# An S5 scan beside a GeGLU on one core: third row block of w_up loaded before x's third tile, and that tile summed by two engines and turned later

## The chip, the cores and the metric

The kernel runs on one core of a Trainium2 chip. The time is device microseconds of one execution; what is compared is the median of several. The kernel before was run three times: 178.42, 178.84 and 178.85 us, median 178.84. A profile is one more execution, with every engine's instructions recorded: TensorE (PE, its weight loads PEld), VectorE (DVE), ScalarE (ACT), GpSimd (POOL), and SyncE (SP), which here issues every transfer.

## What is computed

x is 2048 tokens by 512 channels, in bf16. The normalised x goes through two branches, a diagonal complex recurrence over the tokens (S5) and a gated feed-forward net, and the two are multiplied and added to x:

```python
def _layernorm(x, axis=-1, eps=1e-5):
    m = jnp.mean(x, axis=axis, keepdims=True)
    v = jnp.var(x, axis=axis, keepdims=True)
    return (x - m) / jnp.sqrt(v + eps)
...
    Bu = jnp.einsum("bld,pd->blp", x + 0j, B_bar)
    for t in range(L):
        h = Lam_bar[None, :] * h + Bu[:, t, :]
    y = 2.0 * jnp.einsum("blp,dp->bld", hseq, Cmat).real + x * Dskip[None, None, :]
...
def _B_ref(x, w_gate, w_up, w_down):
    return (_gelu(x @ w_gate) * (x @ w_up)) @ w_down
...
    xn = _layernorm(x, axis=-1)
    s = _A_ref(xn, ...)
    g = _silu(_B_ref(xn, B_w_gate, B_w_up, B_w_down))
    return x + s * g
```

w_gate and w_up are 512 by 1376, w_down is 1376 by 512.

## The kernel before

The tokens are worked in four slabs of 512, each of four tiles of 128 tokens. For each slab the kernel makes the gate and up products, their product turned by a transposing DMA (atT), the product with w_down, the projection by B, the scan (VectorE), and the projection by C. Everything is a step in a list, and the step numbers in the table ORDER fix the order of the instructions: each engine runs its own instructions strictly in that order. SP does the same with the transfers, so a transfer that waits holds back all that are issued behind it.

The change lies in the head, the first 11 us, where slab 0 has to start before x and the weights are all there. x's tiles 0 to 3 (`load_x`, L221) and the 128-row blocks of w_up (`load_w`, L210; its first 1024 columns) are loaded one after the other, in the order x0, x1, w_up block 0, block 1, x2, block 2, block 3; then three small parameter vectors (pv, L234), w_up's other columns, x3 and w_gate. The transfers take their completion semaphores in turn from eight (DMAHW0 to DMAHW7), so a later one waits for the one eight places earlier.

For tiles 0 to 2 the mean is taken off first (`center`, L335), so that the products can start before the variance is known; the variance's factor rs is applied when the products leave PSUM. `center` of tile 0 splits the token sum between ScalarE (192 columns) and VectorE (320 columns). For tiles 1 and 2 ScalarE sums all 512 columns (L350) and VectorE subtracts (L351). `squares` (L354) sums the squares on ScalarE. TensorE turns the centred tile (`head_t`, L305, its transposes L328 into two PSUM banks, which VectorE and ScalarE copy into W, L330 and L331). Then come the row products (`up_rows`, L383): a step `up_rows(m, k)` multiplies tile m's k-th 128 channels with block k of w_up, two 128x512 matmuls into two banks, accumulated over k. There are twelve such steps for the three tiles. Between them lies the parameters' turn (L604: pv against an identity), whose result VectorE copies out (pf, L606), and from which GpSimd makes dt (L607) and later rho (L611) by powers, and VectorE the angles of the rotation tables. GpSimd also makes rs for each tile (L289 to L292). With tile 3's rs VectorE scales tile 3 (L360), and SP issues the first transposing DMA (xnT, L367), behind it those of B (BT, L240), of the first gate product (atT, L468), and the load of w_down (wd, L684).

After the row products TensorE goes on with w_up's last 352 columns and with w_gate (`first_w`, matmuls L421), then with the projection by B (L550) and the product with w_down (L484).

Of the kernel before, what the change touches and what calls it, by code (L numbers as in the profile page):

```python
# [10 lines left out]
AF = mybir.ActivationFunctionType  # L11
# [7 lines left out]


ORDER = (
# [23 lines left out]
)  # L45


# [33 lines left out]
def kernel(  # L81
# [46 lines left out]
    def sb(name, shape, dt=BF16):  # L128
        return consts.tile(shape, dt, name=name)
# [80 lines left out]
    def load_w(nm, k0, k1, c0, c1, end, landed):  # L210

        w, r = w_of[nm]
        dma_sp(end, landed, lambda: nc.sync.dma_start(out=w[:, k0:k1, c0:c1], in_=r[:, k0:k1, c0:c1]),  # L213
               [(nm, k, c) for k in range(k0, k1) for c in range(3) if c0 <= CH[c][0] < c1])
# [6 lines left out]
    def load_x(m, end, landed):  # L221
        dma_sp(end, landed, lambda: nc.sync.dma_start(out=x_tok[:, m, :], in_=x_r[:, m, :]), [("x", 0, m)])  # L222
# [4 lines left out]
    load_x(1, 1.59, 3.31)  # L227
    load_w("wu", 0, 1, 0, W2, 2.06, 4.3)
    load_w("wu", 1, 2, 0, W2, 2.53, 5.0)
    load_x(2, 3.0, 5.3)  # L230
    load_w("wu", 2, 3, 0, W2, 3.5, 6.0)
    load_w("wu", 3, 4, 0, W2, 4.0, 6.7)
    for i, v in enumerate((A_log_dt, A_Lambda_im, A_Lambda_re)):
        dma_sp(4.4 + 0.4 * i, 7.0, lambda i=i, v=v: nc.sync.dma_start(out=pv[4 * i : 4 * i + 4, :], in_=v.rearrange("(k p) -> k p", p=P)), [("pv", i)])  # L234
# [37 lines left out]
    nb = sb("nb", [P, NS, M], FP32)  # L272
    ma = sb("ma", [P, M], FP32)
    mb = sb("mb", [P, 1], FP32)
    ss = sb("ss", [P, M], FP32)

    def stats(m):
# [57 lines left out]
    def center(m):  # L335

        x = x_tok[:, m, :]
        if m == 0:
            c = 320
            acts(D - c, lambda: act(out=junk()[:, 0 : D - c], in_=x[:, c:D], func=AF.Copy, scale=1.0 / D, accum_out=mb[:, 0:1]),  # L340
                 [("x", 0, 0)], ["mb"], ptr=1, rank=400.0)
            dve(c, lambda: V.tensor_scalar(out=yg[0][:, 0:c], in0=x[:, 0:c], scalar1=1.0 / D, scalar2=None, op0=ALU.mult, op1=ALU.add,
                                           accum_out=ma[:, 0:1]), [("x", 0, 0)], [("yg", 0, 0), ("ma", 0)], base=0.15, rank=400.0, after=early)
            for i in range(2):
                hc = slice(i * HD, (i + 1) * HD)
                head.append(dve(256, lambda hc=hc: V.tensor_scalar(out=xn[0][:, hc], in0=x[:, hc], scalar1=ma[:, 0:1], scalar2=mb[:, 0:1], op0=ALU.subtract, op1=ALU.subtract),
                                [("x", 0, 0), ("ma", 0), "mb"], [("xc", 0, i)], rate=2.3, rank=400.0, after=head[-1:]))
            return
        nmean, key = ma[:, m : m + 1], ("ma", m)
        sums0.append(acts(512, lambda: act(out=junk()[:], in_=x, func=AF.Copy, scale=-1.0 / D, accum_out=nmean), [("x", 0, m)], [key], ptr=2, rank=400.0 - 20 * m))  # L350
        dve(512, lambda: V.tensor_scalar(out=xn[m], in0=x, scalar1=nmean, scalar2=None, op0=ALU.add),  # L351
            [("x", 0, m), key], [("xc", m, 0), ("xc", m, 1)], rate=2.3, rank=330.0 - 20 * m)
# [492 lines left out]
```

## Time and profile before

| | |
|---|---|
| median of three runs | 178.84 us (178.42 to 178.85) |
| the profiled execution's own time | 178.47 us |
| its span | 176.7 us |
| TensorE busy | 171.4 us, 97% |
| VectorE busy | 156.7 us, 89% |
| ScalarE busy | 124.0 us, 70% |
| GpSimd busy | 11.3 us, 6% |

The span runs from the first to the last recorded instruction; the execution's own time is 1.8 us longer. Times in the profile are us from the span's start. A row of a timeline reads: start, length, engine, line, operation, what it writes from what it reads, shapes, how many are merged; in brackets how long the engine was idle before and what ended that. Matmuls are pipelined, so the length of a merged row includes the last one's drain, and the pace is read from the distance of starts. "SPq" is SP issuing a transfer; how long the transfer takes until its completion is seen is told apart from that, as the time from issue to landing.

### The profile page before, as it was taken

The page shows a single profiled execution, that of the slowest core. Times are in us where ns is not written, and L with a number is a line of the kernel's source. Part 1 is how long each engine was busy: PE and PEld are TensorE (multiplying, and loading weights), DVE is VectorE, ACT ScalarE, POOL GpSimd, SP SyncE. Part 2 cuts the span into 40 slices and gives each one's busy share as a digit, 9 for nine tenths or more (in the row PEclk, how much of TensorE's full clock was granted, in tenths as well). Part 3 has the DMA queues.
Part 4 walks back from the last instruction along what each step waited for, and adds up shares of the span by engine and source line. Part 5 has one row for each costly group of instructions (what it writes and reads, how often), then busy time and mean ns, then how long its engine had stood idle before and what let it go on. Part 6 is the DMA issues. An engine that isn't in the chain of part 4 may idle for free.

```text
span 176.7 us, 2407 instructions
## 1 busy us (share of the span) xinstructions
PE 171.4 (97%) x830; PEld 82.1 (46%) x846; DVE 156.7 (89%) x254; ACT 124.0 (70%) x238; POOL 11.3 (6%) x25
## 2 busy tenths in 40 slices
PE   8999999999999999999999999999999999999992
PEld 2454554444455544444455454444444455444451
DVE  3578999999799994999979999899999999999764
ACT  5679989959999999799578855373158618582240
POOL 2282030000200000000040000000000000000000
PEclk9999999999999999999999999999999999999999
DMA  5999999999000809423000074194000006526112
GB/s 164 292 334 252 171 221 293 219 256 191 0 0 0 200 7 182 99 83 57 0 0 6 31 148 83 34 189 85 0 0 0 0 30 145 83 57 136 42 59 77
DMA packets 48355, 18.66 MB, mean 106 GB/s; under 512 B 40312, under 2 KB 47832, under 8 KB 48344
## 3 DMA queue, kind: packets, MB, share of 16 engines
q1 hardware_dynamic: 48344, 18.52, 48.2%
q8 instruction: 6, 0.10, 0.2%
q14 instruction: 5, 0.04, 0.1%
HBM read 6.46 MB, written 2.10 MB: 48 GB/s over the span
## 4 chain that ended last, share of the span: by engine, by line
PE 93%; DMA 2%; DVE 1%; SPq 1%; issue 1%; DVEq 0%
PE ring L452 31%; PE ring L484 21%; PE ring L550 16%; PE ybank L500 15%; PE ring L421 5%; PE ybank L421 2%; DMA wu<-in_B_w_up_dram 2%; PE ring L391 2%; DVE yg L505 1%; SPq L222 1%; DVE junk L511 1%; SPq L213 0%; PE ring L328 0%; DVEq L505 0%; PE ybank L604 0%
## 5 line engine op out<-in xcount | busy, mean ns | idle before, releaser
L452 PEld LDWEIGHTS <-xnT 128*128 128x128 bf16 x288 | 28.2, 98 | 28.4
L484 PE MATMUL ring<-wd,atT 128*128 128x512 bf16 (+1 forms) x171 | 38.9, 379 | 0.3
L452 PE MATMUL ring<-wg,xnT 128*128 128x512 bf16 (+1 forms) x142 | 31.4, 356 | 0.1
L452 PE MATMUL ring<-wu,xnT 128*128 128x512 bf16 (+1 forms) x142 | 31.2, 356 | 0.1
L550 PE MATMUL ring<-xnT,BT 128*128 128x512 bf16 x128 | 30.1, 379 | 0.0
L581 DVE TENSOR_TENSOR_SCAN Fs<-rho,ini,W 128x512 bf16<-128x512 f32 x24 | 29.7, 1271 | 0.1
L455 ACT ACTIVATE ub<-ring 128x512 bf16<-128x512 f32 (+1 forms) x36 | 19.2, 555 | 13.6 <-PE ring L452 13.5
L500 PE MATMUL ybank<-C,hst 128*128 128x512 bf16 x115 | 27.3, 379 | 0.3
L484 PEld LDWEIGHTS <-atT 128*128 128x128 bf16 (+1 forms) x176 | 17.2, 98 | 20.8
L552 ACT ACTIVATE U<-ring 128x512 bf16<-128x512 f32 x32 | 18.1, 599 | 7.5 <-PE ring L550 7.5
L455 ACT ACTIVATE gt<-ring 128x512 bf16<-128x512 f32 (+1 forms) x36 | 19.5, 555 | 3.7 <-PE ring L452 3.5
L500 PEld LDWEIGHTS <-hst 128*128 128x128 bf16 x136 | 13.3, 98 | 14.0
L487 ACT ACTIVATE g<-ring 128x512 f32<-128x512 f32 x16 | 9.4, 595 | 14.2 <-PE ring L484 14.2
L550 PEld LDWEIGHTS <-BT 128*128 128x128 bf16 x128 | 12.5, 98 | 14.7
L562 DVE TENSOR_TENSOR Q<-U,tab 128x4096 bf16<-128x4096 bf16 x8 | 18.3, 2290 | 0.9 <-ACT tab L646 0.7
L562 DVE TENSOR_TENSOR Q<-Fs,tab 128x4096 bf16<-128x4096 bf16 x8 | 18.3, 2287 | 0.1
L505 DVE TENSOR_TENSOR yg<-ybank,g 128x512 bf16<-128x512 f32 x15 | 10.2, 685 | 5.8 <-PE ybank L500 5.7
L763 ACT ACTIVATE junk<-x_tok 128x512 bf16<-128x512 bf16 x16 | 10.0, 631 | 1.5 <-DMA x_tok<-in_A_x_dram 1.5
L496 ACT ACTIVATE ybank<-sk 128x512 f32<-128x512 bf16 x15 | 9.0, 603 | 1.7 <-DVE yg L505 1.6
L768 ACT ACTIVATE xna<-x_tok,nb,rs 128x512 bf16<-128x512 bf16 x12 | 9.6, 813 | 0.0
L581 DVE TENSOR_TENSOR_SCAN Fs<-rho,W 128x512 bf16<-128x512 f32 x8 | 9.3, 1210 | 0.1
L461 DVE TENSOR_TENSOR at<-gt,ub 128x1024 bf16<-128x1024 bf16 x12 | 8.2, 684 | 0.0
(143 smaller groups left out, 170.2 us busy)
## 6 DMA issues: line engine op xcount, KB each, us to landing
x_tok<-in_A_x_dram SPq DMA_DIRECT2D x3, 512.0 KB, 4.4
out_dram<-ot SPq DMA_DIRECT2D x12, 128.0 KB, 2.1
wd<-in_B_w_down_dram SPq DMA_DIRECT2D x1, 1280.0 KB, 6.9
wu<-in_B_w_up_dram SPq DMA_DIRECT2D x4, 256.0 KB, 3.6
wg<-in_B_w_gate_dram SPq DMA_DIRECT2D x1, 864.0 KB, 7.2
x_tok<-in_A_x_dram SPq DMA_DIRECT2D x4, 128.0 KB, 4.2
wg<-in_B_w_gate_dram SPq DMA_DIRECT2D x1, 512.0 KB, 5.2
wu<-in_B_w_up_dram SPq DMA_DIRECT2D x1, 352.0 KB, 4.7
```

Of the source, the lines that this page charges most:

```text
L421: T.matmul(ps[:, 0 : b - a], lhsT=lhs(k), rhs=wt[:, k, a:b], start=(k == 0), stop=(k == KT - 1))
L452: T.matmul(ps[:, 0 : b - a], lhsT=xnT[:, s % 2, m, k, :], rhs=wt[:, k, a:b], start=(k == 0), stop=(k == KT - 1))
L455: acts(b - a, lambda: act(out=dst[:, a:b], in_=ps[:, 0 : b - a], func=AF.Copy if up else AF.Gelu_apprx_tanh), [("bank", r)], [key], table= ...
L484: T.matmul(ps[:], lhsT=atT[:fs, k, m * P : (m + 1) * P], rhs=wd[:fs, k, :], start=(k == 0), stop=(k == NFT - 1))
L500: T.matmul(ps, lhsT=hst[s % 2][:, j // NPT, j % NPT, m * P : (m + 1) * P], rhs=C2[:, j // NPT, j % NPT, c0:c1], start=(j == 0 and not seed ...
L505: dve(w, lambda: V.tensor_tensor(out=yg[e][:, c0:c1], in0=ps, in1=g2[gi][:, b, c0:c1], op=ALU.mult), [key, ("g2", gi, b)], [("yg", e, c0)])
L550: T.matmul(ps[:], lhsT=BT[:, ri, k, pt * P : (pt + 1) * P], rhs=xnT[:, s % 2, :, k, :], start=(k == 0), stop=(k == KT - 1))
L552: acts(512, lambda q=q, ri=ri, ps=ps: act(out=U[ui][:, ri, q, :], in_=ps[:], func=AF.Copy), [("bank", r)], [("U", ui, q, ri)])
L562: dve(4096, lambda: V.tensor_tensor(out=Qf, in0=src.unsqueeze(1).to_broadcast(WQ), in1=table, op=ALU.mult), reads, ["Q"], rate=2.0)
L581: pl.add(DVE, 1.12 if s == 0 else 1.185, lambda ri=ri, q=q, pt=pt, first=first: V.tensor_tensor_scan(out=Fs[:, ri, q, :], data0=rho[:, pt ...
L763: acts(512, lambda i=i, fn=fn, sc=sc, m=m: act(out=junk()[:], in_=x_tok[:, s * M + m, :], func=fn, scale=sc, accum_out=sx[:, s, i, m : m + ...
L768: acts(512, lambda m=m: act(out=xn[m], in_=x_tok[:, s * M + m, :], func=AF.Identity, scale=rs[:, s, m : m + 1], bias=nb[:, s, m : m + 1]), ...
```

## The change

The transfers of x2 and of w_up's block 2 change places. Tile 2's sum is split as tile 0's is: ScalarE sums 192 columns into mc, VectorE 320 into md, and VectorE takes off both in one operation; GpSimd adds md and mc into ma, which the squares of tile 2 read. ScalarE now does tile 1's squares ahead of tile 2's sum. The table ORDER is new in its first rows; from there on it is the same order with the step numbers raised by two. All line numbers behind the new lines are 11 higher.

```diff
@@ ORDER
-    25, 26, 1, 29, 27, 24, 22, 23, 21, 2, 3, 4, 5, 38, 19, 20, 17, 18, 0, 6, 30, 31, 32, 39, 7, 8, 9, 10, 11, 28, 33, 35, 34, 36, 37, 52, 53, 55, 56,
+    25, 26, 1, 29, 27, 24, 22, 23, 21, 2, 3, 4, 5, 6, 38, 19, 20, 17, 18, 0, 30, 31, 32, 39, 7, 8, 9, 10, 11, 28, 33, 35, 34, 36, 37, 54, 55, 57, 58,
...
@@ loads
-    load_x(2, 3.0, 5.3)
-    load_w("wu", 2, 3, 0, W2, 3.5, 6.0)
+    load_w("wu", 2, 3, 0, W2, 3.0, 6.0)
+    load_x(2, 3.5, 6.4)
     load_w("wu", 3, 4, 0, W2, 4.0, 6.7)
@@ tiles
+    mc, md = sb("mc", [P, 1], FP32), sb("md", [P, 1], FP32)
@@ def center(m):
+        if m == M - 2:
+            c = 320
+            acts(D - c, lambda: act(out=junk()[:, 0 : D - c], in_=x[:, c:D], func=AF.Copy, scale=-1.0 / D, accum_out=mc[:, 0:1]),
+                 [("x", 0, m)], ["mc"], ptr=1, rank=360.0)
+            dve(c, lambda: V.tensor_scalar(out=yg[0][:, 0:c], in0=x[:, 0:c], scalar1=-1.0 / D, scalar2=None, op0=ALU.mult, op1=ALU.add,
+                                           accum_out=md[:, 0:1]), [("x", 0, m)], [("yg", 0, 0), "md"], base=0.15, rank=360.0)
+            dve(512, lambda: V.tensor_scalar(out=xn[m], in0=x, scalar1=md[:, 0:1], scalar2=mc[:, 0:1], op0=ALU.add, op1=ALU.add),
+                [("x", 0, m), "md", "mc"], [("xc", m, 0), ("xc", m, 1)], rate=2.3, rank=355.0)
+            pool(0.3, lambda: G.tensor_tensor(out=ma[:, m : m + 1], in0=md[:], in1=mc[:], op=ALU.add), ["md", "mc"], [("ma", m)], rank=300.0)
+            return
```

What the new table does is seen in the engines' own order. A row names the line, the instruction, what it writes from what it reads, and in brackets the semaphores that it waits for. On TensorE, from the fifth row product on (block 2 of tile 0, banks ring4 and ring5; tile 1 has ring0 and ring1, tile 2 ring2 and ring3), before:

```order
L391 MATMUL ring4_107<-wu_66,W_87 128x512 [waits DMAHW5_49]
L391 LDWEIGHTS W_87
L391 MATMUL ring5_108<-wu_66,W_87 128x512
L328 LDWEIGHTS xna_90 [waits DVE_49]
L328 MATMUL ring2_105<-ident_111,xna_90 128x128
L328 MATMUL ring3_106<-ident_111,xna_90 128x128
L391 LDWEIGHTS W_87 [waits Activation_49]
L391 MATMUL ring0_103<-wu_66,W_87 128x512
L391 MATMUL ring1_104<-wu_66,W_87 128x512
L604 LDWEIGHTS pv_70 [waits DMAHW7_49,DMAHW1_49,DMAHW0_49]
L604 MATMUL ybank0_109<-ident_111,pv_70 128x12
```

and now (repeated weight loads and the second transpose into a bank are left out in both):

```order
L402 MATMUL ring4_107<-wu_66,W_87 128x512 [waits DMAHW4_49]
L402 MATMUL ring5_108<-wu_66,W_87 128x512
L402 LDWEIGHTS W_87 [waits Activation_49]
L402 MATMUL ring0_103<-wu_66,W_87 128x512
L402 MATMUL ring1_104<-wu_66,W_87 128x512
L402 MATMUL ring4_107<-wu_66,W_87 128x512 [waits DMAHW6_49]
L402 MATMUL ring5_108<-wu_66,W_87 128x512
L329 LDWEIGHTS xna_90 [waits DVE_49]
L329 MATMUL ring2_105<-ident_111,xna_90 128x128
L329 MATMUL ring3_106<-ident_111,xna_90 128x128
L615 LDWEIGHTS pv_70 [waits DMAHW7_49,DMAHW1_49,DMAHW0_49]
L615 MATMUL ybank0_109<-ident_111,pv_70 128x12
```

Tile 2's four transposes stood behind the fifth row product and stand behind the seventh; the two that went ahead of them are block 2 of tile 1 and block 3 of tile 0, which waits for block 3's landing (DMAHW6). One row product (tile 1, block 3; not shown here) still lies between the transposes and the parameters' turn, which so has moved behind two more row products as well. The last eight matmuls are the four of tile 2 alone; before, tile 0's and tile 1's block 3 were among the last twelve.

On SP, the first loads:

```order
 L222 DMA x_tok<-in_A_x_dram 128x512 x2
-L213 DMA wu<-in_B_w_up_dram 128x1024 x2
+L213 DMA wu<-in_B_w_up_dram 128x1024 x3
 L222 DMA x_tok<-in_A_x_dram 128x512
-L213 DMA wu<-in_B_w_up_dram 128x1024 x2
+L213 DMA wu<-in_B_w_up_dram 128x1024
```

The one load of x between those of w_up is tile 2's; it stood behind two blocks and stands behind three. On ScalarE, around tile 2's sum, before:

```order
L331 ACTIVATE W_87<-ybank1_110 128x2x128 [waits PE_49]
L350 ACTIVATE junk1_102,ma_123<-x_tok_63 128x512 [waits DMAHW4_49,Activation_49]
L355 ACTIVATE junk0_101,ss_125<-x_tok_63,ma_123 128x512 [waits Activation_49]
L331 ACTIVATE W_87<-ring3_106 128x2x128 [waits PE_49]
L355 ACTIVATE junk1_102,ss_125<-x_tok_63,ma_123 128x512 [waits Activation_49]
```

and now:

```order
L332 ACTIVATE W_87<-ybank1_110 128x2x128 [waits PE_49]
L366 ACTIVATE junk1_102,ss_127<-x_tok_63,ma_123 128x512 [waits Activation_49]
L352 ACTIVATE junk0_101,mc_125<-x_tok_63 128x192 [waits DMAHW5_49]
L332 ACTIVATE W_87<-ring3_106 128x2x128 [waits PE_49]
L366 ACTIVATE junk1_102,ss_127<-x_tok_63,ma_123 128x512 [waits Pool_49]
```

Tile 1's squares moved ahead of tile 2's sum, which is 192 columns wide now, and tile 2's squares wait for GpSimd's add.

44 rows, old and new, of the table ORDER are left out of this document.

## The prediction

> **What bounds the kernel now.** I read the page first, then TensorE's list of waits over the whole span, then TensorE's timeline in the first 11 us.
>
> ```profile
> span 176.7 us, 2407 instructions
> PE 171.4 (97%) x830; PEld 82.1 (46%) x846; DVE 156.7 (89%) x254; ACT 124.0 (70%) x238; POOL 11.3 (6%) x25
> ```
> ```profile
> PE ybank L299 <- PEq L829: 0.8, 1, 0.8
> PE ring L391 <- DMA wu<-in_B_w_up_dram: 0.4, 1, 0.4
> ```
>
> The second fence is the whole list of TensorE's waits: the program's start, and one wait of 0.4 us for rows of w_up. After that it streams to the end, so a microsecond saved in the head is saved at the end, unless something becomes late that today is just in time. TensorE in the head:
>
> ```profile
> 4.67 1.91 PE L391 MATMUL ring<-wu,W 128*128 128x512 bf16 x8
> ...
> 6.20 0.38 PE L391 MATMUL ring<-wu,W 128*128 128x512 bf16 x1
> ...
> 6.99 0.59 PE L391 MATMUL ring<-wu,W 128*128 128x512 bf16 x2 [0.41 <-DMA wu<-in_B_w_up_dram]
> 7.54 0.40 PE L328 MATMUL ring<-ident,xna 128*128 128x128 bf16 x4
> 7.77 0.59 PE L391 MATMUL ring<-wu,W 128*128 128x512 bf16 x2
> 8.23 1.46 PE L391 MATMUL ring<-wu,W 128*128 128x512 bf16 x6
> ...
> 10.82 0.46 PE L421 MATMUL ybank<-wu,W 128*128 128x352 bf16 x2
> ```
>
> Durations include the drain; the pace is the distance of starts. Twelve matmuls start from 8.23 to 10.82: 2.59 / 12 = 0.216 us each, so a row product (two matmuls) costs 0.43. The eighth matmul starts at 6.20, so the next could start at 6.42; it starts at 6.99: 0.57 lost. Its pair ends its turn at 7.42, and the transposes of tile 2 start at 7.54: 0.12 more. The transposes take 0.23 (7.54 to 7.77); the small parameter product 0.03 (7.77 + 0.43 = 8.20, next start 8.23). Check: 16 x 0.216 + 0.23 + 0.03 + 0.57 + 0.12 = 4.41, and 10.82 - 6.42 = 4.40. **0.69 us is all there is to win**, 0.4% of the span.
>
> **The loads.** Issues by SP's timeline, by the chain of waits (2.11, and 3.06 with its length up to the landing) and by the DMA list's time from issue to landing.
>
> ```profile
> 2.11 0.43 SPq L213
> wu<-in_B_w_up_dram SPq DMA_DIRECT2D x1, 256.0 KB, 3.3
> 2.58 0.43 SPq L222 DMA_DIRECT2D x_tok<-in_A_x_dram  x1
> x_tok<-in_A_x_dram SPq DMA_DIRECT2D x1, 128.0 KB, 3.7
> 3.06 3.88 DMA wu<-in_B_w_up_dram
> 3.53 0.43 SPq L213 DMA_DIRECT2D wu<-in_B_w_up_dram  x1
> wu<-in_B_w_up_dram SPq DMA_DIRECT2D x1, 256.0 KB, 4.1
> ```
>
> Row blocks 1, 2 and 3 of w_up land at 5.41, 6.94 and 7.63, x's tile 2 between them at 6.28. The change swaps tile 2 and block 2. What lies ahead of block 3 is the same set of bytes, so I keep its landing at 7.63. Tile 2 takes the place behind the same bytes that block 2 had: 6.94. Block 2 lands between 6.07 (5.41 plus the 0.66 that it took behind tile 2) and 6.94. Any landing up to 6.77 gives the same sum, because its four matmuls then end before block 3 is there.
>
> **Tile 2's centring.** Tile 0 is already summed by two engines, so its rows price the new form; the last two rows are tile 2's old form.
>
> ```profile
> 2.90 0.49 DVE L342 TENSOR_SCALAR_CACHE_REDUCE yg<-x_tok 128x320 bf16<-128x320 bf16 x1 [1.78 <-DMA x_tok<-in_A_x_dram]
> 3.51 0.60 DVE L346 TENSOR_SCALAR xna<-x_tok,ma,mb 128x256 bf16<-128x256 bf16 x2
> ...
> 6.37 0.63 ACT L350 ACTIVATE junk<-x_tok 128x512 bf16<-128x512 bf16 x1 [1.12 <-DMA x_tok<-in_A_x_dram]
> 7.13 0.35 DVE L351 TENSOR_SCALAR xna<-x_tok,ma 128x512 bf16<-128x512 bf16 x1 [1.26 <-ACT junk L350]
> ```
>
> Old: 7.13 - 6.37 = 0.76 from the sum's start to the centring. New: 3.51 - 2.90 = 0.61. The centring itself stays one 128x512 operation, 0.35, with two scalars for one; tile 0's two-scalar form took 0.30 per 256 columns, so 0.35 to 0.60, and I take 0.35 since the operation, type and width are those of the last row (0.60 would make T below 8.30 instead of 8.11). From its end to the transposes 0.06 (7.48 to 7.54), from landing to the sum 0.09 (6.28 to 6.37). Tile 2 is ready 0.09 + 0.61 + 0.35 + 0.06 = 1.11 after landing: 8.05 by my landing. VectorE's added sum (0.49) lies in its 1.26 of idle time. The squares of tile 1 go ahead of the sum on ScalarE, into its 1.12 idle. GpSimd's new one-column add lies in the 1.83 idle of its row below, and its price, at most the 0.57 of a one-column operation there, is hidden; without that cover it would delay the squares of tile 2 on ScalarE, which nothing reads before the tile's scale.
>
> **TensorE's new head.** Row 2 of both tiles starts at 6.42 or when block 2 lands, and is done before block 3. Row 3 of tile 0 starts at 7.63 + 0.05 (6.94 to 6.99 above) = 7.68 and gives up its turn at 8.11. The transposes need tile 2 at 8.05, so they start at T = 8.11. Then 0.23 + 0.43 + 0.03 and eight matmuls, 1.73: 10.53 against 10.82. **TensorE's term: -0.29**, or T - 8.40 for other T. The old wait goes, but most of it comes back as a wait for block 3.
>
> **What is now late.** The parameter product goes behind T, and a chain hangs on it: parameters, GpSimd's powers, tile 3's scale, and SP, which issues in order, behind that scale.
>
> ```profile
> 8.41 0.17 DVE L606 COPY pf<-ybank 128x12 f32<-128x12 f32 x1
> 8.66 1.02 POOL L607 TENSOR_TENSOR dt__135<-e_t,pf 128x4 f32<-128x4 f32 x1 [1.83 <-DVE pf L606]
> 12.20 0.57 POOL L292 TENSOR_TENSOR rs<-ve,mhalf 128x1 f32<-128x1 f32 x1
> 12.80 0.41 DVE L360 TENSOR_SCALAR xna<-x_tok,mv,rs 128x512 bf16<-128x512 bf16 x1 [0.24 <-POOL rs L292]
> 13.24 2.83 SPq L367 DMA_TRANSPOSE xnT<-xna  x2
> 16.11 2.71 SPq L240 DMA_TRANSPOSE BT<-in_A_B_re_dram  x1
> 18.87 2.90 SPq L240 DMA_TRANSPOSE BT<-in_A_B_im_dram  x1
> 21.18 0.34 DVE L436 TENSOR_TENSOR at<-gt,at 128x352 bf16<-128x352 bf16 x1
> 21.87 1.68 SPq L468 DMA_TRANSPOSE atT<-at  x1
> 23.59 0.58 SPq L684 DMA_DIRECT2D wd<-in_B_w_down_dram  x1
> wd<-in_B_w_down_dram SPq DMA_DIRECT2D x1, 1280.0 KB, 6.9
> BT<-in_A_B_im_dram SPq DMA_TRANSPOSE x1, 5.6
> 24.23 7.07 PE L550 MATMUL ring<-xnT,BT 128*128 128x512 bf16 x32
> 31.13 7.30 PE L484 MATMUL ring<-wd,atT 128*128 128x512 bf16 x32
> 64.91 1.67 SPq L367 DMA_TRANSPOSE xnT<-xna  x1
> ```
>
> The parameter copy follows the transposes by 8.41 - 7.54 = 0.87: T - 7.54 = 0.57 later. GpSimd runs on from there without a gap to tile 3's scale at 12.77, and VectorE waits for it (0.24), so tile 3's scaled rows and SP's first transposing DMA are late by 0.57 too. SP is then back to back: 13.24 + 2.83, 16.11 + 2.71, 18.87 + 2.90, 21.87 + 1.68, 23.59. At the end of it hangs w_down: it lands at 30.49 and TensorE wants it at 31.13, 0.59 to spare with the 0.05 of a wake-up. B's second part lands at 24.47 and is wanted four matmuls after 24.23, at 25.09: 0.57 to spare. With TensorE 0.29 early and SP 0.57 late, both are missed by 0.27 to 0.29; that is the upper bound, and since one wait covers the other it counts once. The lower bound: these issues are slow because the DMA is full (the 16 blocks of xnT took 2.83 here, 1.67 at 64.91), so a late start may be made up on the way; but the atT issue cannot go before VectorE has the product that ends at 21.52, which follows the same late parameters: 22.09 plus 0.04 against 21.87, 0.26 late, and then nothing is missed. So 0 to +0.29; I take the middle of the lateness (0.42), which misses w_down by 0.12. **Sum: -0.29 + 0.12 = -0.17**: the span 176.53, the profiled execution 178.47 becomes 178.30. The median of the runs shown, 178.84, is 0.37 above that execution, hence **178.65** for the median.
>
> VectorE stays late by up to 0.57 until this wait absorbs it:
>
> ```profile
> 47.15 0.75 DVE L739 SCALAR_TENSOR_TENSOR C<-hst,ncre,tF 128x512 bf16<-128x512 bf16 x1 [0.82 <-ACT tF L734]
> ```
>
> **Rivals.** *Both waits go:* transfers overlap, and tile 2 is half a block, so block 3 could be there by 7.24 and tile 2 by 6.61. Then T = 6.42 + 6 x 0.216 = 7.72 and TensorE gains 0.68; the SP chain is 0.18 late, misses w_down by at most 0.27, and the net is -0.41 to -0.68: 178.3. Against it: landings came 0.66 to 0.87 apart whatever the size, so nothing shows block 3 moving. *Slower, tile 2 late:* from the point where it lands after 7.0, T is its landing plus 1.11, and every tenth delays both TensorE and the parameters. With the SP chain fully coupled the net is T - 7.54 - 0.59 = T - 8.13; a landing at 7.4 gives T = 8.51, +0.38, 179.2; at 7.6 it is +0.58. For it: tile 2 took 0.87 behind block 1, the longest step of all, for half the bytes. Against: 7.4 would need 0.46 more than that place gave block 2. *The clock hides it:* the change then does nothing for TensorE.
>
> ```profile
> 1.57 2.20 PE L299 MATMUL ring<-const-bfloat16-1.0 128*128 128x512 bf16 x5
> ```
>
> These five took 0.44 each, against 0.216 from 4.67 on. If the first eight row matmuls ran at 0.44 in some executions, they would last to 8.19, every load would be there in both kernels, and only the four matmuls put ahead of the parameters would count: 0 to +0.3, 179.0. [...]
>
> **Chances.** Forecast (-0.29 to 0): 0.50. Both waits go: 0.25. Tile 2 late: 0.17. Clock: 0.08. A measurement of this kernel tells about 0.3%, 0.54 us, from no change. Past it on the fast side lies most of the second case and a little of the first: 0.22. On the slow side rather more than half of the third and the edges of the others: 0.14. Within: 0.64. The likeliest case's own range is 178.5 to 178.9; the range that takes in the others is 178.1 to 179.2.
>
> **What would show it.** Right: the wait for block 2 gone or under 0.2, a wait for block 3 that ends near 7.7, transposes near 8.1, the first 128x352 product near 10.5, the parameter copy near 9.0, SP's first transposing DMA near 13.8, and a short wait before w_down's or B's first use, or none. Wrong: tile 2 landing past 7.1, block 3 off 7.6 by more than 0.2, or TensorE waiting after 32 us for something that the head did not touch.

## The result and the profile after

The changed kernel takes 179.18 us (median of 13 runs, 178.90 to 180.34), the kernel before 178.72 (13 runs of the same comparison, 178.31 to 178.85): a ratio of 1.0045 with a 95% interval of 1.0027 to 1.0063. It is slower by 0.46 us; the prediction was 178.65 and faster by a little. Of the changed kernel's 13 runs seven lie from 178.90 to 179.18 and six from 179.64 to 180.34. Its profiled execution took 179.69 us, with a span of 177.9 (before: 176.7); it is one of the upper six, and so is the second profile further down (e7, 179.74), so what the lower seven wait for stands in no profile of this kernel. In the table of the experiments two of e3's twelve runs, over 1.5% above its fastest, are left out.

The page of the changed kernel, its first lines, and the whole list of TensorE's waits:

```profile
span 177.9 us, 2409 instructions
PE 172.3 (97%) x830; PEld 82.7 (46%) x846; DVE 157.3 (88%) x256; ACT 123.6 (69%) x238; POOL 11.5 (6%) x26
```
```profile
PE ring L495 <- DMA wd<-in_B_w_down_dram: 0.8, 1, 0.8
PE ybank L300 <- PEq L840: 0.8, 1, 0.8
```

The old wait of 0.4 for w_up is gone, as the change meant, and a wait of 0.8 for w_down stands in its place, 25 us later. TensorE's timeline in the head of the changed kernel:

```profile
4.34 0.42 PE L304 MATMUL ring<-const-bfloat16-1.0 128*128 128x256 bf16 x1
4.55 0.63 PE L329 MATMUL ybank<-ident,xna 128*128 128x128 bf16 x4
4.98 3.77 PE L402 MATMUL ring<-wu,W 128*128 128x512 bf16 x14
8.58 0.39 PE L329 MATMUL ring<-ident,xna 128*128 128x128 bf16 x4
8.80 0.60 PE L402 MATMUL ring<-wu,W 128*128 128x512 bf16 x2
9.23 0.17 PE L615 MATMUL ybank<-ident,pv 128*128 128x12 bf16 x1
10.99 1.36 PE L432 MATMUL ybank<-wu,W 128*128 128x352 bf16 x8
```

All fourteen matmuls that are now ahead of tile 2's transposes run without a wait, yet they need 3.60 us (4.98 to 8.58) where 14 x 0.216 = 3.02 were reckoned: the first ones ran at half pace. The same view in a narrower window has the starts:

```profile
4.98 1.06 PE L402 MATMUL ring<-wu,W 128*128 128x512 bf16 x2
5.83 0.75 PE L402 MATMUL ring<-wu,W 128*128 128x512 bf16 x2
```

The third start is 0.85 behind the first, 0.42 each. The pace doubled in the middle of the row products here. In the profile before it had doubled before 4.29, where the same small matmul took 0.27 and not 0.42. "The clock is late" stands below for this: the first row products 0.42 apart and not 0.216. The profile's own column of the granted clock does not show the step; it reads 1.00 from 2 to 6 us in both. The trace's records of that clock do: the first, at 1.00, begins at 3.50 us in before and at 6.15 in the changed kernel. So the transposes start at 8.58, against 8.11 predicted and 7.54 before, and everything that hangs on the parameters is 1.06 late and not 0.57. VectorE and SP in the changed kernel, with TensorE's first product with w_down:

```profile
7.14 0.49 DVE L354 TENSOR_SCALAR_CACHE_REDUCE yg<-x_tok 128x320 bf16<-128x320 bf16 x1 [1.02 <-DMA x_tok<-in_A_x_dram]
7.74 0.41 DVE L356 TENSOR_SCALAR xna<-x_tok,md,mc 128x512 bf16<-128x512 bf16 x1
9.47 0.17 DVE L617 COPY pf<-ybank 128x12 f32<-128x12 f32 x1
13.86 0.41 DVE L371 TENSOR_SCALAR xna<-x_tok,mv,rs 128x512 bf16<-128x512 bf16 x1 [0.24 <-POOL rs L293]
```
```profile
14.30 2.84 SPq L378 DMA_TRANSPOSE xnT<-xna  x2
17.18 4.14 SPq L240 DMA_TRANSPOSE BT<-in_A_B_re_dram  x1
21.37 2.04 SPq L240 DMA_TRANSPOSE BT<-in_A_B_im_dram  x1
23.51 1.78 SPq L479 DMA_TRANSPOSE atT<-at  x1
25.33 0.58 SPq L695 DMA_DIRECT2D wd<-in_B_w_down_dram  x1
```
```profile
32.27 7.29 PE L495 MATMUL ring<-wd,atT 128*128 128x512 bf16 x32 [0.80 <-DMA wd<-in_B_w_down_dram]
```

Read down the queue: the parameter copy is 1.06 late (8.41 before), tile 3's scale 1.06 (12.80), SP's first transposing DMA 1.06 (13.24), and w_down's issue 1.74 (23.59), since B's first part took 4.14 and not 2.71 (the second gives back 0.86 of that, 2.04 for 2.90). The load takes its 6.9 us as before, lands at 32.23, and TensorE starts 1.14 late (31.13). Of the 1.14, TensorE brings 0.17 from the head (10.99 against 10.82) and the wait adds the rest; that is nearly the whole difference of the spans, 1.2.

### The profile page after: what moved, and what is told of

Read it like the earlier page. It is cut to its first block, busy times and chain, and to the rows that moved or that the text cites. A ratio compares the mean times of both kernels' runs of the same rounds, so it can differ in the third digit from the quotient of the medians.

```text
span 177.9 us, 2409 instructions
## 1 busy us (share of the span) xinstructions
PE 172.3 (97%) x830; PEld 82.7 (46%) x846; DVE 157.3 (88%) x256; ACT 123.6 (69%) x238; POOL 11.5 (6%) x26
## 4 chain that ended last, share of the span: by engine, by line
PE 81%; ACT 12%; DMA 2%; DVE 1%; issue 1%; SPq 1%; DVEq 0%
PE ring L463 27%; PE ring L495 16%; PE ybank L511 14%; PE ring L561 10%; PE ring L432 5%; ACT U L563 4%; PE ring L402 3%; DMA x_tok<-in_A_x_dram 2%; ACT junk L774 2%; PE ybank L432 2%; PE ring L300 1%; ACT xna L779 1%; ACT tF L745 1%; ACT gt L466 1%; DVE yg L516 1%
```

## The experiments

Two theories stood at the start. **Theory 1**: the parameters, now behind tile 2's transposes, hold back GpSimd, tile 3's scale and SP's queue, and w_down at its end. **Theory 2**: the swapped loads disturb the transfers. The two later questions (theories 1a and 1b, F1 and F2) are in the expectations. All times are medians of twelve runs (thirteen in the first comparison; e3 ten, e8 eight, e12 six, e14 seven, e17 nine) beside runs of the kernel before on the same chip, whose median was 178.69 for e1 to e8, 178.71 for e9 to e11, 178.75 for e12 to e14 and 179.09 for e15 to e17. The ratio is to those runs; it need not be the quotient of the two medians (e14: 1.0033). The other columns are from the one profiled execution of each kernel: the start of tile 2's transposes, of the first 128x352 product, of SP's first transposing DMA, of w_down's issue, and TensorE's wait for w_down.

| kernel | us | ratio, 95% interval | transp. | 128x352 | xnT | w_down | wait |
|---|---|---|---|---|---|---|---|
| before | 178.72 | 1 | 7.54 | 10.82 | 13.24 | 23.59 | 0 |
| e8 before again | 178.65 | 0.9997 (0.9978 to 1.0016) | 7.62 | 10.97 | 13.40 | 23.64 | 0 |
| changed | 179.18 | 1.0045 (1.0027 to 1.0063) | 8.58 | 10.99 | 14.30 | 25.33 | 0.8 |
| e7 changed again | 179.24 | 1.0028 (1.0009 to 1.0047) | 8.31 | 10.72 | 14.04 | 25.00 | 1.1 |
| e1 | 179.03 | 1.0010 (0.9983 to 1.0037) | 8.12 | 10.52 | 13.13 | 23.92 | 0.4 |
| e2 | 179.50 | 1.0030 (1.0005 to 1.0055) | 7.39 | 10.69 | 13.97 | 24.35 | 0.2 |
| e3 | 179.99 | 1.0074 (1.0041 to 1.0107) | 8.73 | 11.14 | 14.45 | 22.95 | 0 |
| e4 | 179.38 | 1.0033 (1.0008 to 1.0058) | 8.19 | 10.60 | 13.92 | 23.91 | 0.3 |
| e5 | 179.09 | 1.0024 (0.9999 to 1.0048) | 8.51 | 10.91 | 13.39 | 23.59 | 0 |
| e6 | 179.02 | 1.0026 (1.0000 to 1.0052) | 8.08 | 10.47 | 13.31 | 24.31 | 0.8 |
| e9 | 179.08 | 1.0026 (1.0000 to 1.0053) | 8.07 | 10.48 | 13.79 | 23.95 | 0 |
| e10 | 178.76 | 1.0003 (0.9983 to 1.0023) | 7.93 | 11.21 | 13.63 | 23.60 | 0 |
| e11 | 179.04 | 1.0013 (0.9994 to 1.0032) | 8.64 | 11.03 | 12.89 | 23.41 | 0 |
| e12 | 179.79 | 1.0057 (1.0037 to 1.0078) | 8.00 | 10.40 | 13.04 | 23.75 | 0 |
| e13 | 179.28 | 1.0031 (1.0014 to 1.0048) | 7.63 | 10.93 | 13.35 | 24.53 | 0 |
| e14 | 179.34 | 1.0054 (1.0027 to 1.0081) | 7.98 | 10.38 | 13.70 | 24.34 | 0 |
| e15 | 179.50 | 1.0021 (0.9998 to 1.0045) | 8.36 | 10.76 | 12.61 | 23.76 | 0 |
| e16 | 179.25 | 1.0002 (0.9979 to 1.0025) | 7.87 | 11.14 | 13.56 | 23.82 | 0 |
| e17 | 180.51 | 1.0064 (1.0032 to 1.0096) | 8.54 | 10.94 | 14.25 | 24.86 | 0 |

### e1 to e4: the late parameters or the swapped loads

**e1**, the changed kernel with the parameters early (the order of TensorE's and VectorE's instructions):

```
 PE
+L615 MATMUL ybank<-ident,pv 128x12
 L329 MATMUL ring<-ident,xna 128x128
...
-L615 MATMUL ybank<-ident,pv 128x12
 DVE
+L617 COPY pf<-ybank 128x12
 L331 COPY W<-ring 128x2x128
 L374 TENSOR_SCALAR xna<-xna,rs 128x512
-L617 COPY pf<-ybank 128x12
```

> The changed kernel, with the parameter product moved ahead of tile 2's transposes (behind the seventh row product) and its copy ahead of VectorE's copy of the turned tile; nothing else. Theory 1 (late parameters: the loss is the parameter product's new place, which reaches TensorE through GpSimd's powers, tile 3's scale, SP's queue and the load of w_down): parameter copy near 8.4 us or, if TensorE's clock rises late, 8.8; SP's first transposing DMA at 13.2 to 13.7; the 0.8 us wait for w_down gone or under 0.2; time 178.2 to 178.6, ratio to the kernel before 0.997 to 1.000. Theory 2 (the swapped loads themselves disturb the transfers, the parameters are bystanders): still slower than before by 0.3% or more, near 179.2.

**e2**, the kernel before with nothing but the parameter product two row products (four matmuls) later:

```
 PE
+L391 MATMUL ring<-wu,W 128x512 x4
 L604 MATMUL ybank<-ident,pv 128x12
-L391 MATMUL ring<-wu,W 128x512 x4
```

> The kernel before, with only the parameter product moved behind two more row products (0.86 us of TensorE's time); loads, sums and transposes as before. Theory 1: parameter copy near 9.3, SP's first transposing DMA near 14.1, a wait for w_down of 0.2 to 0.9 us that the kernel before has not, time 179.0 to 179.6, ratio 1.001 to 1.005. Theory 2: no change, 178.7, no wait for w_down.

**e3**, the changed kernel with w_down's load one place earlier in SP's queue:

```
 SP
 L240 DMA_TRANSPOSE BT<-in_A_B_im_dram
+L695 DMA wd<-in_B_w_down_dram
 L479 DMA_TRANSPOSE atT<-at
-L695 DMA wd<-in_B_w_down_dram
```

> The changed kernel, with the load of w_down issued one place earlier on SP, ahead of the first transposing DMA of the gate product (atT); nothing else. Theory 1: w_down is issued near 23.4 instead of 25.3, lands near 30.5 to 31, the wait for it goes; what is left is TensorE's head, so 178.3 to 178.7, unless atT, now behind w_down, becomes the next wait (then 179 or more). Theory 2: whatever holds the queue holds w_down too; the gain is under 0.3 us, 179.0.

**e4**, the changed kernel with x's tile 2 loaded ahead of block 2 again:

```diff
-... 2, 3, 4, 5, 6, 38, ...
+... 2, 3, 4, 6, 5, 38, ...
```

> The changed kernel with the two loads swapped back (x's tile 2 ahead of w_up's third block), all else as changed: split sum, transposes and parameters behind two more row products. Theory 1: the parameters are as late as in the changed kernel (copy near 9.2 to 9.5), the wait for w_down stays at 0.5 to 1.0, time 179.0 to 179.4. Theory 2: without the swap the transfers run as before, no wait for w_down, 178.6 to 178.8.

e2 is the clearest: without one line of the change but the late parameters, the kernel before is slower, by 0.30% (0.05 to 0.55), SP starts 0.73 later and a wait for w_down of 0.2 appears, where the prediction's slack of 0.59 would have let through about 0.17. e1 puts the parameters back; its time, 179.03, is above the 178.2 to 178.6 expected, its interval holds both no change and a loss of 0.3%, and in its profile a wait of 0.4 for w_down is left. Alone it settles nothing. e4 undoes the swap, and the loss stays, so the swap is not what makes the changed kernel slower; that it does delay one transfer, w_gate, is seen under e9. In e3 the wait for w_down is gone, a wait of 0.5 for atT has its place, and the time is worse: the wait goes from one transfer of the queue to the next.

### e5 to e8: where the lateness can be cut, and a second look

**e5** takes other work out of the way of tile 3's scale and leaves the parameters late:

```
 POOL
+L292, L293 (rs of tile 1)
 L358 TENSOR_TENSOR ma<-md,mc
 L618 TENSOR_TENSOR dt<-e_t,pf
-L292, L293 (rs of tile 1)
 DVE
 L617 COPY pf<-ybank
+L281, L282 (statistics of tile 3)
 L619 ... L627
-L281, L282 (statistics of tile 3)
```

> The changed kernel with two pieces of other work moved out of the way of tile 3's scale: GpSimd's power for tile 1 goes ahead of the parameters' power into GpSimd's idle time before it, and VectorE's statistics of tile 3 go into its idle time behind the parameter copy. TensorE's and SP's orders stay, and the parameters stay late (copy near 9.5). Theory 1a, the loss runs from the late parameters over GpSimd's queue and tile 3's scale into SP's queue and from there into w_down's landing: tile 3's scale at about 12.8 and not 13.86, SP's first transposing DMA at about 13.2, w_down issued between 23.6 and 24.2, TensorE's wait for it under 0.2; the time falls by 0.6 to 0.8 against the changed kernel, to within 0.15 of the kernel before. Theory 1b, the late parameters hurt over their own users (angles, tables, VectorE's later work): w_down's issue moves, but the time stays within 0.2 of the changed kernel. Theory 2, TensorE's own head is longer in most executions (late clock, fourteen products in a row): TensorE's first 128x352 product stays near 11.0 and the time keeps 0.2 to 0.4 of the loss.

**e6** is e5 with e1's edit as well.

> The same two moves, and the parameter product ahead of tile 2's transposes with its copy ahead of tile 2's copy. Theory 1a: SP's first transposing DMA at about 12.5 to 13.0, no wait for w_down, nothing late that the kernel before had on time, so what the change wins in TensorE's head is left over: 0 to 0.3 us faster than before. Theory 2: the head wins nothing, so the time equals the kernel before within 0.15; a time above before by 0.3 or more would mean that another wait comes from the change that neither theory has.

**e7** and **e8** are the two kernels unchanged.

> The changed kernel unchanged, beside the others on this chip, and a second profiled execution of it. Both theories: 0.4 to 0.9 us above before. The second profile tells whether TensorE's clock rises at the same place (near 6.0, transposes near 8.6) or earlier (then transposes near 8.1 to 8.2, SP's first transposing DMA near 13.9 and the wait for w_down 0.2 to 0.4).

> The kernel before, a second profiled execution. If the place where TensorE's clock rises changes from execution to execution, the first row products may run at 0.43 here; they then fill the wait for w_up's third rows, the transposes stay at 7.4 to 7.6, and the parameter copy within 0.2 of 8.41. If the place belongs to the kernel, the products run at 0.216 from the first one on, as in the first profile.

e5's profiled execution (178.58 us) is what theory 1a asked for. VectorE's and SP's rows:

```profile
9.39 0.17 DVE L617 COPY pf<-ybank 128x12 f32<-128x12 f32 x1
12.95 0.41 DVE L371 TENSOR_SCALAR xna<-x_tok,mv,rs 128x512 bf16<-128x512 bf16 x1
```
```profile
13.39 3.52 SPq L378 DMA_TRANSPOSE xnT<-xna  x2
...
23.59 0.85 SPq L695 DMA_DIRECT2D wd<-in_B_w_down_dram  x1
```

The parameters are as late as in the changed kernel, tile 3's scale by 0.15 only, w_down is issued at the old 23.59, and TensorE waits for nothing: a span of 176.8. So in this execution the path is GpSimd's powers, tile 3's scale, SP; the parameters' other users cost nothing. The median does not bear it out: 179.09, only 0.15 under e7, where 0.6 to 0.8 were expected. Six of its twelve runs lie from 178.46 to 178.95 and five from 179.60 to 180.31. The second kind is not in its profile; it is in e6's (179.81), whose TensorE waits stand here, the second list that of the weight loads:

```profile
PE ring L495 <- DMA wd<-in_B_w_down_dram: 0.8, 1, 0.8
...
```
```profile
...
PEld L432 <- DMA wg<-in_B_w_gate_dram: 0.9, 2, 0.5
```

In e6 SP starts at 13.31, as early as in before, and TensorE has won its 0.35 in the head (10.47 against 10.82). It gives them back to w_gate: B's first product starts at 24.28, against 24.23. Then the transposing DMAs take longer (w_down issued at 24.31), and w_down is waited for though nothing of the change is late.

e8 shows what a late clock does to before. TensorE's timeline of its second execution:

```profile
4.38 0.42 PE L303 MATMUL ring<-const-bfloat16-1.0 128*128 128x256 bf16 x1
...
5.13 2.66 PE L391 MATMUL ring<-wu,W 128*128 128x512 bf16 x10
7.62 0.39 PE L328 MATMUL ring<-ident,xna 128*128 128x128 bf16 x4
```

The clock is late here too, and the slow matmuls fill the time in which the first execution waited 0.41 for w_up: the transposes start 0.08 later, the span is 0.2 longer. The cover has a limit: in e10 and e16, whose heads are those of before, the pace doubles later still (ten row matmuls from 5.01 and 5.00, the transposes behind them at 7.93 and 7.87; 5.13 and 7.62 in e8). In the changed kernel's two profiles there is no such wait to fill, and the lateness passes on in full to the transposes, the parameters and SP; e7's profile has it again (8.31, and a wait of 1.1):

```profile
16.91 4.18 SPq L240 DMA_TRANSPOSE BT<-in_A_B_re_dram  x1
...
25.00 0.81 SPq L695 DMA_DIRECT2D wd<-in_B_w_down_dram  x1
```

### e9 to e11: w_down in two loads

```diff
-dma_start(out=wd[:, 0 : NFT - 1, :], in_=wd_r)
+[dma_start(out=wd[:, k0:k1, :], in_=wd_r[:, k0:k1, :]) for k0, k1 in ((0, 6), (6, NFT - 1))]
```

**e9** is the changed kernel with it, **e10** the kernel before, **e11** e6.

> The changed kernel, w_down's one load of ten row blocks cut into two at the same place of SP's queue, six blocks and four; everything else stays, the parameters stay late. TensorE's first product with w_down then needs only the first 768 KB; the rest is wanted six matmuls (1.3 us) later. Theory 1, the loss is the wait for w_down's single landing behind the late queue: the wait is gone or under 0.2, and the time falls by 0.5 to 0.8 us, to 178.5 to 178.8. Theory 2, the loss is TensorE's head (more products ahead of the transposes, late clock): the wait goes but 0.2 to 0.4 us stays. If the wait only changes its name (atT, or the second part of w_down), the time stays within 0.2 of the changed kernel.

> The same cut in the kernel before, which had 0.59 us to spare at w_down in its first profiled execution and no wait in its second. Theory 1: no gain, within 0.15 us of before (a little less in executions where the loads are slow); a gain of 0.3 or more would mean that before waits for w_down too in most executions.

> The same cut in the kernel of e6 (changed kernel with the parameters early and tile 3's scale early), whose profile had TensorE 0.35 ahead of before at the first 128x352 product (10.47 against 10.82), then 0.9 us of weight-load waits for w_gate and 0.8 us for w_down. Theory 1 with the loads as the floor: the wait for w_down goes, the one for w_gate stays, so it equals before within 0.2 us or is up to 0.2 faster. If the head's 0.35 us can be kept, 178.3 to 178.4.

The wait for w_down is gone in e9 and e11, and e10, its control, is unmoved. In e9's profile the clock is up early (the 128x256 matmul at 4.34 takes 0.29), and TensorE's head is as short as the prediction reckoned. TensorE, and its weight loads' waits:

```profile
5.06 3.18 PE L402 MATMUL ring<-wu,W 128*128 128x512 bf16 x14
8.07 0.39 PE L329 MATMUL ring<-ident,xna 128*128 128x128 bf16 x4
...
10.48 1.36 PE L432 MATMUL ybank<-wu,W 128*128 128x352 bf16 x8
...
12.66 0.61 PE L432 MATMUL ring<-wg,W 128*128 128x512 bf16 x2 [0.22 <-DMA wg<-in_B_w_gate_dram]
```
```profile
PEld L432 <- DMA wg<-in_B_w_gate_dram: 0.9, 2, 0.6
```
```profile
24.29 7.07 PE L561 MATMUL ring<-xnT,BT 128*128 128x512 bf16 x32
```

The transposes start at 8.07 (predicted 8.11) and the first 128x352 product at 10.48 (10.53): the head's 0.34 is there. At w_gate it is lost, and B's product starts at 24.29, 0.06 behind before. SP and w_gate's first load, in before and in e9:

```profile
6.30 1.04 SPq L213 DMA_DIRECT2D wg<-in_B_w_gate_dram  x2
wg<-in_B_w_gate_dram SPq DMA_DIRECT2D x1, 512.0 KB, 5.2
```
```profile
6.57 0.93 SPq L213 DMA_DIRECT2D wg<-in_B_w_gate_dram  x2
wg<-in_B_w_gate_dram SPq DMA_DIRECT2D x1, 512.0 KB, 6.0
```

This is the swap's doing in part. w_gate's first load comes eight places behind the fifth transfer and is issued when that one has landed: behind x's tile 2 in before (landed 6.28, issued 6.30), behind block 2 now (6.55 and 6.57 in e9, 6.80 and 6.81 in the changed kernel's first profile). In before it lands at 11.5, a microsecond ahead of its use at 12.61; in e9 at 12.6, where TensorE wants it near 12.27. Over the kernels with w_gate's loads whole it lands at 11.4 to 12.0 in the old order of loads and at 11.7 to 12.7 in the new one; why it also takes longer in some is not shown. e4 has the old order: TensorE, 0.22 ahead at the first 128x352 product, waits for no w_gate and starts B's product at 24.01, still 0.22 ahead. No run has the old order together with early parameters, so whether that gain could be kept stays open.

The median of e9, 179.08, is within 0.2 of the changed kernel, so the wait has changed its place: five of twelve runs are at 179.68 and more.

### e12 to e17: can the head's gain be kept

**e12** is e11, **e13** e10 and **e14** e9, each with w_gate's two loads cut as well:

```diff
-load_w("wg", 0, KT, 0, TS, 5.5, 11.0)
-load_w("wg", 0, KT, TS, F, 6.0, 13.5)
+load_w("wg", 0, KT, 0, TS, 5.5, 11.0, [(0, 2, 0, TS), (2, KT, 0, TS)])
+load_w("wg", 0, KT, TS, F, 6.0, 13.5, [(0, KT, TS, W2), (0, KT, W2, F)])
```

> The kernel of e11 with w_gate's two loads cut too: the first 512 KB into two halves of the rows, the other 864 KB into its columns 512 to 1024 and the rest. The profile of e9 showed TensorE's head gain in full (first 128x352 product at 10.48 against 10.82) and lost again at w_gate: 0.22 us of wait and 0.9 us of weight loads that waited for it, B's product at 24.29 against 24.23. Theory F1, what is lost there is lost because whole loads are waited for: w_gate's waits go, TensorE reaches B's first product near 23.9, and the time falls to 178.2 to 178.5, below before by 0.2 to 0.5. Theory F2, the loads as a whole are the floor (the DMA has no more to give, and only the waits change places): the time stays at 178.6 to 179.1, and later waits (w_down's second part, atT, B) appear.

> The kernel before with the same three loads cut. Its profiles show no wait for w_gate or w_down, so both theories: within 0.2 us of before, a little less in executions where the loads are slow. A gain as large as that of e12 would mean that cutting helps by itself and not through the change.

> The changed kernel, parameters late as it has them, with the same three loads cut. F1: no wait for w_gate and w_down, and the time at before or up to 0.3 below it in executions where TensorE's clock is up early, at before where it is late. F2: 0.2 to 0.5 above before, as e9.

In e12 TensorE is ahead for the first time beyond w_gate, at B (23.80 against 24.23) and at w_down (30.71 against 31.13), and then loses it behind ScalarE. TensorE and ScalarE of e12, then the same row of ScalarE before:

```profile
23.80 7.07 PE L561 MATMUL ring<-xnT,BT 128*128 128x512 bf16 x32
30.71 7.30 PE L495 MATMUL ring<-wd,atT 128*128 128x512 bf16 x32
...
50.02 2.60 PE L463 MATMUL ring<-wg,xnT 128*128 128x512 bf16 x12 [0.29 <-ACT gt L466]
```
```profile
38.63 0.63 ACT L774 ACTIVATE junk<-x_tok 128x512 bf16<-128x512 bf16 x1 [2.37 <-DMA x_tok<-in_A_x_dram]
```
```profile
38.17 0.63 ACT L763 ACTIVATE junk<-x_tok 128x512 bf16<-128x512 bf16 x1 [1.48 <-DMA x_tok<-in_A_x_dram]
```

ScalarE's statistics of slab 2 wait for the fourth transfer behind w_down in SP's queue, issued at 34.18 against 33.76; ScalarE is 0.46 late from there on, its evictions of slab 1's gate products too, and TensorE, 0.42 ahead until then, starts twelve matmuls at 50.02 that before starts at 49.88:

```profile
49.88 2.49 PE L452 MATMUL ring<-wg,xnT 128*128 128x512 bf16 x12
```

The control e13 is slower too, by 0.31% (0.14 to 0.48), where 0.2 us at most was expected, and its TensorE has the same wait of 0.29 for the gate's eviction. So the cuts bring that loss, and e12 does not show that the change does. Part of it lies behind all queues: from the start of VectorE's last operation to the end of the span the kernels with one load cut take some 0.17 us longer than before, and those with three 0.31 (174.02 to 176.7 in before, 174.41 to 177.2 in e10, 174.76 to 177.7 in e13). At the end SP reads the completion semaphores one after the other, some 0.06 us apart (174.77, 174.84, 174.90 in before); the last output's is the last one in before, has three behind it in e10 and five in e13. e12's median is above e13's, though the intervals overlap; no gain of the head is in the time.

**e15**, **e16** and **e17** are e12, the kernel before and e14, with slab 2's load one place earlier in SP's queue:

```
 SP
 L479 DMA_TRANSPOSE atT<-at
+L217 DMA x_tok<-in_A_x_dram 128x4x512
 L378 DMA_TRANSPOSE xnT<-xna 128x16x128
-L217 DMA x_tok<-in_A_x_dram 128x4x512
```

> The kernel of e12 with the load of x's slab 2 one place earlier in SP's queue, ahead of the transposing DMA of slab 1's rows. In e12's profile TensorE kept its 0.42 us up to 43.68 (44.10 before) and lost 1.2 us from 47.8 to 53.4 behind ScalarE, whose statistics of slab 2 started at 38.63 against 38.17 because the load was issued at 34.18 against 33.76. Theory F1, it was only that: ScalarE's statistics start before 37.5, the wait for the gate's eviction goes, and the time is 178.2 to 178.5, below before. Theory F2, the floor is SP's queue as a whole: another wait takes its place (slab 1's transposed rows, atT) and the time stays at or above before.

> The kernel before with slab 2's load at that earlier place and nothing else. Its profile has no wait there, so both theories: within 0.2 us of before. If it gains 0.3 or more, before waits there too in many executions.

> The kernel of e14 (the changed kernel, parameters late, three loads cut) with slab 2's load at that earlier place. F1: at before or up to 0.3 below. F2: 0.2 to 0.6 above before, as e14.

The wait for the gate's eviction goes in e15, and others take its place. ScalarE in e15 waits for C, where it has no wait in before; TensorE in e17 waits for slab 1's turned rows:

```profile
46.67 1.15 ACT L745 ACTIVATE tF<-hst,cim 128x1024 f32<-128x1024 bf16 x1 [1.08 <-DMA hst<-in_A_C_im_dram]
```
```profile
PE ring L561 <- DMA xnT<-xna: 0.9, 1, 0.9
```

Neither goes below before. The control e16 has the same wait for C in its profile (1.06), and its weight loads wait 0.5 for slab 1's turned rows as e15's do, so these come from moving slab 2's load and not from the change; its median cannot be told from that of before. That is the outcome of F2: a move of one transfer between 13 and 45 us makes another late. No version here beats the kernel before; e1 and e11 come nearest, within what can be told from no change.

## Why the prediction was wrong

**The loads** were right in the main. Block 2 lands at 6.8 (2.58 + 4.2), in the stretch from 6.07 to 6.94 but at its late end; tile 2 at 7.1 (6.94 predicted), block 3 at 7.8 (7.63). TensorE waited for none of them in the profiled execution, not even for block 3. What the prediction did not look at is the transfer whose issue block 2's landing releases, w_gate's first.

**Tile 2's centring** was right: from the start of the sum to the centring 0.60 (0.61 predicted), and the operation with two scalars took 0.41, nearer to the 0.35 that was taken than to its bound of 0.60.

**TensorE's term, -0.29,** comes out with an early clock (e9: 10.48 - 10.82 = -0.34) and is wrong in both profiles of the changed kernel (+0.17 and -0.10). In e9 the agreement is partly luck: the row products start at 5.06 and not at 4.67, and so never meet the wait for block 3 that the sum had; e12's, from 4.67, do (block 3 lands at 7.50, its first matmul starts at 7.55). What failed is the pace: the sum took 0.216 for every row matmul from the first on, from a profile in which the clock happened to be up by then. The rival "The clock hides it" named this and put 179.0 on it, at a chance of 0.08; of the four profiles of the two kernels, three have the late clock. That the step moves, which one profile could not show, these four do: the pace doubles before 3.60 in the first profile of before and between 5.1 and 6.2 in the other three. The rival's own count, the four matmuls put ahead of the parameters, fits: between the late-clock profiles, e8's and the changed kernel's first, SP's first transposing DMA moves by 0.90 (13.40 to 14.30), four matmuls being 0.86. What it lacked is what the queue then adds.

**What is now late: +0.12, bounded by +0.29.** This is the step that turned the sign. The chain was named link by link, and each link is in the profile, with 1.06 for 0.57 as the copy's lateness. But the lower bound, and with it the middle, rested on "a late start may be made up on the way". Sometimes it is (e4: 0.68 late at SP's first transposing DMA, 0.32 at w_down), but in e2 it arrived whole (0.73 and 0.76), and in the changed kernel's two profiles it grew (1.06 to 1.74, 0.80 to 1.41). The upper bound took the duration of the transposing DMAs from the one execution that was shown, so it left no room for that. From SP's first transposing DMA to w_down's issue it took 10.35 us there and 10.24 in e8, but 11.03 and 10.96 in the changed kernel's two, and 11.00 in e6. The late start does not bring that longer stretch with it: it is 10.38 in e2, 9.99 in e4 and 10.16 in e9, which start 0.55 to 0.73 late. In place of 0.12 stands a wait of 0.8, or 1.1 in e7.

**What was left out** is where the gain itself can be lost. The prediction wrote that a microsecond saved in the head is saved at the end "unless something becomes late that today is just in time", and looked at w_down and B alone. w_gate, which had a microsecond of margin in before, has none in the new order of loads (e9, e6). With the parameters early as well (e1, e6, e11) nothing is gained that can be told; e11's profile has no shorter head to begin with (11.03), as its loads came late.

That the late parameters alone make the kernel before slower is shown by e2's runs (0.05% to 0.55%). That their path is tile 3's scale and SP's queue is shown in e5's one profile; its median got back only 0.15 us. So the rest of the loss is open, and with it two things. Why B's first part is issued in 2.7 to 2.9 us in the two profiles of before and in 4.1 to 4.2 in those of the changed kernel was not settled: e3, e4 and e14, all with the changed kernel's late parameters, have 3.30, 3.42 and 3.84; e5, with them too, has 2.64; e6, with a start as in before, has 3.61, and e13, the kernel before with cut loads, 3.87. And the upper runs of e5 and e9 were not caught in a profile, so that they wait where e6 does is an inference.

## What to carry to other kernels

Before a wait on the busiest engine is removed, list every later transfer with its margin, for that engine running earlier by the gain, not only the ones behind the moved step; in e6 and e9 the gain was taken back at w_gate, the first of them that had none. Where two transfers change places, look also at the later ones that are released by their landings. A wait in the head can be cover: in e8 it took up nearly all of the slow matmuls. And a step that a serial queue hangs on, however small (0.03 us of TensorE), should not be put behind a stretch whose length differs between executions.

## What was not expected of the hardware

**The point at which TensorE's pace doubles moves by over 2 us.** In e11 a 128x256 matmul takes 0.27 at 3.56 already; in the changed kernel the row matmuls from 4.98 to 5.83 still start 0.42 apart.

**One stretch of transposing DMAs moves under half the bytes.** The rows of a table by stretch, with the DMA's busy share and GB/s last, of before:

```profile
12.00:16.00 4.00, 3.95 (x21) 1.96 (x20) 2.85 (x22) 3.98 (x11) 2.24 (x5) 1.00 1.15 308
16.00:20.00 4.00, 4.00 (x24) 2.15 (x22) 3.93 (x7) 3.99 (x7) 0.00 (x0) 1.00 1.09 138
20.00:24.00 4.00, 3.95 (x21) 2.03 (x21) 3.93 (x10) 4.00 (x10) 0.70 (x2) 1.00 1.29 260
```

The DMA is busy throughout in all three (its share is 1.15, 1.09 and 1.29). From 16 to 20, where mainly transposing transfers run, it moves 138 GB/s (145 in the changed kernel), against 308 just before. From 20 to 24 the transfers are transposing ones too, and it moves 260 (170 in the changed kernel), so transposing alone does not make the slow stretch; what does is not shown.
